# VectorE's order within a step of the dense layers, and PSUM banks of their own for the first step's last products

## The chip, the cores and the metric

The kernel runs on one core of a Trainium2 chip. The metric is the time of one execution on the device in microseconds (us); several executions are timed, and their median counts. TensorE is called PE below (its weight loads PEld), VectorE DVE, ScalarE ACT, GpSimd POOL, SyncE SP.

## The reference

Three stages, one after the other: a block attention over 2 x 768 tokens, a mixture of 8 experts (512 to 1024 to 512), and two dense layers with a piecewise quadratic gate between them. The change lies in the third stage alone:

```python
def _moe2_ref(x, w_in, w_out):            # x 1536 x 512, w_in 512 x 2048, w_out 2048 x 512
    h = x @ w_in
    neg = h <= -1.0
    pos = h >= 1.0
    g = np.where(pos, h, np.where(neg, 0.0, (h + 1.0) ** 2 / 4.0))
    return g @ w_out
```

## The kernel before

The dense layers begin 333.5 us into the span, when the experts' last matmul has been issued, and run to its end. They go through 16 steps (the loop over `s` in `run`): steps 0 to 7 take eight pairs of 128 hidden features for the first 768 tokens, steps 8 to 15 the same pairs for the other 768.

**Products.** A step computes 256 features of h for 768 tokens as a 2 x 2 by 2 x 2 block product with seven products in place of eight (the Strassen-Winograd scheme). Each is six matmuls (L1010) of 128 x 384, since every operand is split into a high part (`ah`, `yh`) and a remainder (`al`, `yl`). Product j of a step goes into a PSUM tile `ph`, of which there are two. Products 0, 1, 4 and 6 begin a tile; 2 adds onto 0's, 3 onto 1's, 5 onto 4's. So between them stand readers:

- `x1` (ACT, L1130) copies product 0; product 2 may write onto it only then.
- `u2` (DVE, L1132) is product 1 plus x1; product 3 may write only then.
- `u3` (DVE, L1132) is products 1 and 3 plus x1. Product 4 takes the tile that u3 has read.
- c22 (DVE, L1139) is product 4 plus u3; product 5 may write only then. c12 is product 5's tile plus u2, c21 is product 6 plus u3. c11 is product 0's tile after product 2, with no add.

**Gates.** Each of c11, c22, c12, c21 then passes through `gate`, a generator in three parts: relu and square on ACT (L1018, L1019); a clamp on DVE (L1021) and the high part `gh` on ACT (L1023); the remainder `gl` on DVE (L1026). `advance()` runs the next part of every open gate. It is called once for each product, so a gate's parts are issued one product apart or more.

**Outer products.** After each product, five (after the last six) matmuls of 128 x 512 (L1043) of the step before are issued: `gh` and `gl` times the split rows of w_out (`wh`, `wl`), added up over eight steps in six PSUM tiles `po0` to `po5`. These and the two `ph` fill PSUM. The four blocks of a step are used up in the order c11 (`po0` to `po2`), c12 (`po3` to `po5`), c21, c22.

**The other work in a step.** DVE makes four sums of w_in's blocks for the next step (`sums`, L977: S0 to S3 below, 128 x 256 each); ACT and POOL split the seven left operands of the next step (`side`, `ah` L987, `al` L988), where sides 1, 3, 4 and 5 read S1, S2, S0 and S3; `split` makes `wh` on ACT and `wl` on DVE (steps 0 to 5) or POOL (from step 6 on; L1001). In steps 1 to 6 `fill` converts the weights that are still missing from 64-bit to 32-bit floats, three DVE operations (L931, L933, L935) for each half tile, seven operations in a step; the third one issues the next load on SP. Step 6 also makes four combinations of the second half's tokens on DVE (`second`, L1075 to L1081), and step 7 splits them (`renew`, ACT L1088 and DVE L1090; the last one in step 8). In step 8 the first half's results are stored.

Nothing is scheduled by a planner: each engine executes its instructions in the order in which this Python code issues them. For steps 1 to 15 that order on DVE is, by product (work that a step doesn't have falls out):

| product | DVE, in order |
|---|---|
| 0 | gl(c12), clamp(c21) of the step before; S0, S1, S2, S3; one fill |
| 1 | u2; gl(c21); one fill |
| 2 | one fill |
| 3 | u3; clamp(c11); one fill |
| 4 | c22; gl(c11); wl of the first half; one fill |
| 5 | c12; clamp(c22); one fill |
| 6 | c21; gl(c22), clamp(c12); wl of the second half; one fill |

Of the kernel before, what the change touches and what calls it, by code (L numbers as in the profile page):

```python
# [8 lines left out]
F32 = mybir.dt.float32  # L9
# [4 lines left out]
OP = mybir.AluOpType  # L14
# [4 lines left out]
B, H, S, D = 2, 8, 768, 64  # L19
# [24 lines left out]
HALF = 384  # L44
# [759 lines left out]
def run_experts(router, ex, ff, plan=PLAN):  # L804
# [67 lines left out]
    for n, _ in enumerate(run):  # L872
        if n % TAIL == 0:
            next(conversions, None)
# [3 lines left out]
class FeedForward:  # L878
# [89 lines left out]
        sub(self.L[:, 3:7, :, v], R[:, :, :, at + 96:at + 192], self.H[:, 3:7, :, v].bitcast(F32))  # L968
        return todo

    def sums(self, p):

        nc, S, a = self.nc, self.S, self.pair(p)
        a11, a12, a21, a22 = (a[:, i, 256 * c:256 * c + 256] for i in range(2) for c in range(2))
        for j, (x, y, op) in enumerate(((a21, a22, OP.add), (S[:, 0], a11, OP.subtract), (a11, a21, OP.subtract),
                                        (a12, S[:, 1], OP.subtract))):
            nc.vector.tensor_tensor(S[:, j], x, y, op=op)  # L977

    def side(self, s, j):

# [10 lines left out]
    def split(self, s, i):  # L991

        nc = self.nc
        x = self.pair(s % self.PAIRS)[:, i, 512:]
        h = self.ww.tile([128, 512], F32R, name="wh")
        l = self.ww.tile([128, 512], F32R, name="wl")
        self.W[s, i] = h, l
        nc.scalar.activation(h, x, AF.Copy)
        if s < 6:
            yield  # L1000
        (nc.vector if s < 6 else nc.gpsimd).tensor_tensor(l, x, h.bitcast(F32), op=OP.subtract)  # L1001

    def product(self, s, j, p, first):

# [87 lines left out]
    def run(self, ctx):  # L1092
        nc, tc = self.nc, self.tc
# [10 lines left out]
        x1, u2, u3 = (self.st.tile([128, HALF], F32, name=n) for n in ("x1", "u2", "u3"))  # L1104
        P = self.PAIRS
        lower, upper = range(3), range(3, 6)
        order = ((0, 0, lower), (0, 1, upper), (1, 0, lower), (1, 1, upper))
        gates, renewed, rest = [], iter(()), iter(())

        def advance():  # L1110
            for g in list(gates):
                if next(g, 0) == 0:
                    gates.remove(g)

        for s in range(2 * P):
            outer = self.outer(s - 1, order) if s else iter(())
            for j, (_, kind) in enumerate(self.STEPS):
                if j in (0, 1, 4, 6):
                    p = self.pp.tile([128, HALF], F32, name="ph")
                    first = True  # L1120
                    if j == 0:
                        px = p
                    elif j == 1:
                        py = p
                else:
                    p = {2: px, 3: py, 5: p}[j]
                    first = False
                self.product(s, j, p, first)
                if j == 0:
                    nc.scalar.activation(x1, p, AF.Copy)  # L1130
                elif kind in ("u2", "u3"):
                    nc.vector.tensor_tensor(u2 if kind == "u2" else u3, p, x1, op=OP.add)  # L1132
                elif kind == "c11":
                    advance()
                    gates.append(self.gate((s, 0, 0), p))
                    next(gates[-1])
                else:
                    c = self.wk.tile([128, HALF], F32, name="c")
                    nc.vector.tensor_tensor(c, p, u2 if kind == "c12" else u3, op=OP.add)  # L1139
                    advance()  # L1140
                    gates.append(self.gate((s, int(kind[1]) - 1, int(kind[2]) - 1), c))
                    next(gates[-1])
                if j in (0, 1, 3):
                    advance()
                next(rest, None)
                for _ in range((12 if j == 6 else 4) if s == 2 * P - 1 else (6 if j == 6 else 5)):
                    next(outer, None)
                if s + 1 < 2 * P:
                    if j == 0:
                        while self.done < min(4 * (s + 1) + 2, len(self.halves)) and s + 1 < P:  # L1150
                            next(self.fill)
                        self.sums((s + 1) % P)
                    self.side(s + 1, j)
                if j in (3, 5):
                    while self.done < 4 * s + 4 and s < P:
                        next(self.fill)
                    rest = self.split(s, j // 5)
                    next(rest, None)
                if s:
                    next(self.fill, None)  # L1160
                if s == P - 2 and j in (1, 3, 5, 6):
                    self.second((1, 3, 5, 6).index(j))
                next(renewed, None)
                if s == P - 1:
                    renewed = self.renew(j)
                    next(renewed)
        for _ in range(2):
            advance()
        for t in (3, 4, 5, 0, 1, 2):
            h = t // 3  # L1170
# [59 lines left out]
```

## Time and profile before

| | us |
|---|---|
| median of 3 runs | 607.24 (605.71 to 609.76) |
| the profiled execution: its time | 608.52 |
| the profiled execution: its span, first to last instruction | 606.7 |
| of it before the dense layers' first matmul | 333.5 |

All times of rows below are from the start of the span of this one execution. A stall of an engine is the idle time ahead of an instruction; the profile names what ended it. A matmul row's length is longer than its pitch, since matmuls overlap: 128 x 384 matmuls start 0.17 to 0.18 us apart when nothing holds them. A row marked `[0.65 <-DVE u L1132]` had 0.65 us of idle time before it, which ended with that DVE operation.

### The profile page before, as it was taken

Reading aid. Unit: us, or ns where it says so; the run is one execution under the profiler, and the core shown is the slowest. Engines: PE = TensorE matmul, PEld = TensorE weight load, DVE = VectorE, ACT = ScalarE, POOL = GpSimd, SP = SyncE. Lnnn points to the kernel's source line nnn. Section 1 sums busy time; section 2 is a strip of 40 time slices with the busy share of each in tenths; the row PEclk is TensorE's granted clock in tenths of the full one; section 3 lists DMA queues with packets and bytes.
Section 4 is the critical chain, followed back from the end, with each engine's and each line's share of the span. In section 5 each row is a group of like instructions: output and inputs, shape, how many; then the busy total and the mean of one; then the engine's idle time right before and its main releaser. Section 6 shows DMA issues by size and latency. Waiting matters only on the chain.

```text
span 606.7 us, 11467 instructions
## 1 busy us (share of the span) xinstructions
PE 578.9 (95%) x4316; PEld 486.5 (80%) x4316; DVE 422.7 (70%) x1094; ACT 277.4 (46%) x645; POOL 176.6 (29%) x273
## 2 busy tenths in 40 slices
PE   6799998999999999999999889999999999999996
PEld 4568683478888888899999778888787889888884
DVE  6887865753664656620888799999999677777761
ACT  5666660021222222222321765556578566666653
POOL 5412100110101101110400333343365575555534
PEclk9999998999999999999999999999999899999999
DMA  9999023497837539498567222221000110000002
GB/s 214 185 202 205 26 89 123 62 314 231 273 92 244 197 108 284 167 184 228 189 222 245 54 70 70 70 79 61 1 0 1 68 38 2 0 1 0 2 1 104
DMA packets 84073, 71.42 MB, mean 118 GB/s; under 512 B 42546, under 2 KB 71218, under 8 KB 84018
## 3 DMA queue, kind: packets, MB, share of 16 engines
q1 hardware_dynamic: 81506, 64.38, 39.2%
q0 software_dynamic: 1984, 6.29, 3.7%
q8 instruction: 34, 0.56, 0.4%
q14 instruction: 21, 0.17, 0.1%
q10 hardware_dynamic: 528, 0.02, 0.0%
HBM read 64.38 MB, written 6.30 MB: 116 GB/s over the span
## 4 chain that ended last, share of the span: by engine, by line
PE 73%; DVE 18%; ACT 3%; issue 3%; POOL 1%; DMA 0%; POOLq 0%; DVEq 0%
PE acc L783 15%; PE acc L792 15%; PE ph L1010 14%; PE po L1043 11%; DVE sums L977 2%; PE rt L566 2%; DVE u L1021 2%; PE px L716 2%; PE po L313 2%; DVE gl L1026 2%; PE pt L299 2%; PE ps L275 2%; DVE u L1132 1%; DVE slot L933 1%; PE ptr L168 1%
## 5 line engine op out<-in xcount | busy, mean ns | idle before, releaser
L783 PE MATMUL acc<-xt,slot 128*128 128x192 f32 x512 | 95.5, 334 | 0.6 <-ACT xt L765 0.6
L792 PE MATMUL acc<-ht,slot 128*128 128x192 f32 x512 | 94.7, 333 | 0.0
L1010 PE MATMUL ph<-yh,ah 128*128 128x384 f32 x224 | 78.8, 352 | 9.4 <-DVE u L1132 7.7
L783 PEld LDWEIGHTS acc<-xt,slot 128*128 128x128 f32 x512 | 82.1, 190 | 1.7 <-ACT xt L765 0.8
L792 PEld LDWEIGHTS acc<-ht,slot 128*128 128x128 f32 x512 | 82.3, 190 | 0.8
L988 POOL TENSOR_TENSOR al<-sums,ah 128x256 fp32r<-128x256 f32 x64 | 53.4, 835 | 80.8 <-ACT ah L987 64.8
L1010 PE MATMUL ph<-yh,al 128*128 128x384 f32 x224 | 75.8, 338 | 0.0
L1043 PE MATMUL po<-wh,gh 128*128 128x512 f32 x192 | 75.8, 395 | 0.0
L1043 PE MATMUL po<-wl,gh 128*128 128x512 f32 x192 | 75.8, 395 | 0.0
L1043 PE MATMUL po<-wh,gl 128*128 128x512 f32 x192 | 75.5, 393 | 0.0
L1010 PE MATMUL ph<-yl,ah 128*128 128x384 f32 x224 | 75.5, 337 | 0.0
L988 POOL TENSOR_TENSOR al<-slot,ah 128x256 fp32r<-128x256 f32 x48 | 43.2, 900 | 100.3 <-ACT ah L987 92.7
L724 POOL DMA_INDIRECT xg<-xdram,idx x16 | 15.0, 936 | 184.1 <-ACT idx L695 94.3
L1023 ACT ACTIVATE gh<-u 128x384 fp32r<-128x384 f32 x64 | 33.6, 525 | 73.1 <-DVE u L1021 72.6
L1010 PEld LDWEIGHTS ph<-yh,ah 128*128 128x128 f32 x224 | 42.2, 188 | 22.3 <-DVE u L1132 16.3
L1026 DVE TENSOR_TENSOR gl<-u,gh 128x384 fp32r<-128x384 f32 x64 | 50.6, 791 | 4.7 <-ACT gh L1023 4.7
L787 ACT ACTIVATE ht<-acc 128x192 f32<-128x192 f32 x64 | 21.1, 330 | 66.6 <-PE acc L783 66.6
L1010 PEld LDWEIGHTS ph<-yl,ah 128*128 128x128 f32 x224 | 42.3, 189 | 3.2
L1139 DVE TENSOR_TENSOR c<-ph,u 128x384 f32<-128x384 f32 x48 | 26.7, 556 | 26.0 <-PE ph L1010 25.3
L1010 PEld LDWEIGHTS ph<-yh,al 128*128 128x128 f32 x224 | 42.2, 189 | 0.0
L1043 PEld LDWEIGHTS po<-wh,gl 128*128 128x128 f32 x192 | 36.2, 189 | 6.1 <-DVE gl L1026 0.4
L1043 PEld LDWEIGHTS po<-wh,gh 128*128 128x128 f32 x192 | 36.4, 189 | 5.1
(228 smaller groups left out, 998.6 us busy)
## 6 DMA issues: line engine op xcount, KB each, us to landing
slot<-in_moe_w_dram SPq DMA_DIRECT2D x31, 1024.0 KB, 8.8
raw<-in_moe_w_in_dram SPq DMA_DIRECT2D x16, 512.0 KB, 4.1
raw<-in_moe_w_out_dram SPq DMA_DIRECT2D x16, 512.0 KB, 3.4
vw<-in_v_dram SPq DMA_DIRECT2D x20, 192.0 KB, 5.2
nat<-in_k_dram SPq DMA_DIRECT2D x12, 256.0 KB, 4.7
nat<-in_q_dram SPq DMA_DIRECT2D x12, 256.0 KB, 5.4
xdram<-xs SPq DMA_DIRECT2D x12, 256.0 KB, 3.1
slot<-in_moe_w_dram SPq DMA_DIRECT2D x2, 512.0 KB, 3.5
```

Of the source, the lines that this page charges most:

```text
L275: nc.tensor.matmul(s[a][64 * w:64 * w + 64, c], QT[b * G + i // 2][r, c, n:n + 64], KW[b][r, i // 2, c, n // 64], start=False, stop=True, ...
L299: nc.tensor.transpose(pt[:, c], pr[:, c], ident)
L724: nc.gpsimd.indirect_dma_start(out=self.XG[k][:, h], out_offset=None, in_=self.x, in_offset=bass.IndirectOffsetOnAxis(ap=idx[:, h:h + 1], ...
L783: nc.tensor.matmul(p, w[:, c, f % 4 * 128:f % 4 * 128 + 128], xt[:, c], start=(c == 0), stop=(c == 3))
L787: nc.scalar.activation(ht[:, f], p, AF.Relu)
L792: nc.tensor.matmul(p, w[:, f, c % 2 * 128:c % 2 * 128 + 128], ht[:, f], start=(f == 0), stop=(f == 7))
L988: nc.gpsimd.tensor_tensor(l, x, h.bitcast(F32), op=OP.subtract)
L1010: nc.tensor.matmul(p, w[:, 128 * c:128 * c + 128], y[:, b, c], start=first and n == 0, stop=n == 5, skip_group_check=True)
L1023: nc.scalar.activation(gh, u, AF.Copy)
L1026: nc.vector.tensor_tensor(gl, u, gh.bitcast(F32), op=OP.subtract)
L1043: nc.tensor.matmul(self.po[t], x[:, c], w, start=(self.left[t] == 6 * self.PAIRS - 1), stop=(self.left[t] == 0))
L1139: nc.vector.tensor_tensor(c, p, u2 if kind == "c12" else u3, op=OP.add)
```

## The change

`sums` can issue some of its four operations. In `run`:

- S0, S1, S2, S3 are issued at products 0, 1, 3 and 5, no longer all at product 0; a side waits in the loop until its sum has been issued.
- `advance()` comes behind u2 and u3 as before, but ahead of the c22, c12 and c21 adds, no longer behind them.
- c21's gate is only put on the list at product 6; its relu and square are issued by the next step's first `advance()`, its clamp at product 1, its gl at product 2. After the loop there are three rounds of `advance()` in place of two.
- The seven fills of a step are issued 1, 0, 3, 1, 1, 1, 0 by product in place of one each.
- Step 0 takes its products in the order 0, 1, 4, 2, 3, 5, 6; products 4, 5 and 6 go into `po3`, `po4` and `po5`, with no adding of 5 onto 4. c12 is then made by two adds (product 4 plus u2 ahead of time, later product 5). Both `wl` of step 0 are made on POOL, and `split` comes at the third and the fifth product.
- Step 1 uses up step 0's blocks in the order c11, c22, c12, c21, so that `po3` to `po5` are first needed for c22.

On DVE, steps 1 to 15 then have this order:

| product | DVE, in order |
|---|---|
| 0 | gl(c12) of the step before; S0; one fill |
| 1 | u2; clamp(c21); S1 |
| 2 | gl(c21); three fills |
| 3 | u3; clamp(c11); S2; one fill |
| 4 | gl(c11); c22; wl of the first half; one fill |
| 5 | clamp(c22); c12; S3; one fill |
| 6 | gl(c22), clamp(c12); c21; wl of the second half |

```diff
--- before.py
+++ after.py
@@ -968,13 +968,14 @@
         sub(self.L[:, 3:7, :, v], R[:, :, :, at + 96:at + 192], self.H[:, 3:7, :, v].bitcast(F32))
         return todo
 
-    def sums(self, p):
-
-        nc, S, a = self.nc, self.S, self.pair(p)
+    def sums(self, p, which=range(4)):
+
+        S, a = self.S, self.pair(p)
         a11, a12, a21, a22 = (a[:, i, 256 * c:256 * c + 256] for i in range(2) for c in range(2))
-        for j, (x, y, op) in enumerate(((a21, a22, OP.add), (S[:, 0], a11, OP.subtract), (a11, a21, OP.subtract),
-                                        (a12, S[:, 1], OP.subtract))):
-            nc.vector.tensor_tensor(S[:, j], x, y, op=op)
+        todo = ((a21, a22, OP.add), (S[:, 0], a11, OP.subtract), (a11, a21, OP.subtract), (a12, S[:, 1], OP.subtract))
+        for j in which:
+            x, y, op = todo[j]
+            self.nc.vector.tensor_tensor(S[:, j], x, y, op=op)
 
     def side(self, s, j):
 
@@ -996,9 +997,9 @@
         l = self.ww.tile([128, 512], F32R, name="wl")
         self.W[s, i] = h, l
         nc.scalar.activation(h, x, AF.Copy)
-        if s < 6:
+        if 0 < s < 6:
             yield
-        (nc.vector if s < 6 else nc.gpsimd).tensor_tensor(l, x, h.bitcast(F32), op=OP.subtract)
+        (nc.vector if 0 < s < 6 else nc.gpsimd).tensor_tensor(l, x, h.bitcast(F32), op=OP.subtract)
 
     def product(self, s, j, p, first):
 
@@ -1105,6 +1106,7 @@
         P = self.PAIRS
         lower, upper = range(3), range(3, 6)
         order = ((0, 0, lower), (0, 1, upper), (1, 0, lower), (1, 1, upper))
+        first = ((0, 0, lower), (1, 1, upper), (0, 1, upper), (1, 0, lower))
         gates, renewed, rest = [], iter(()), iter(())
 
         def advance():
@@ -1112,59 +1114,76 @@
                 if next(g, 0) == 0:
                     gates.remove(g)
 
+        def block(s, key, p, other):
+
+            c = self.wk.tile([128, HALF], F32, name="c")
+            nc.vector.tensor_tensor(c, p, other, op=OP.add)
+            if key is None:
+                return c
+            gates.append(self.gate((s,) + key, c))
+            if key != (1, 0):
+                next(gates[-1])
+
         for s in range(2 * P):
-            outer = self.outer(s - 1, order) if s else iter(())
-            for j, (_, kind) in enumerate(self.STEPS):
-                if j in (0, 1, 4, 6):
-                    p = self.pp.tile([128, HALF], F32, name="ph")
-                    first = True
-                    if j == 0:
-                        px = p
-                    elif j == 1:
-                        py = p
+            outer = self.outer(s - 1, first if s == 1 else order) if s else iter(())
+            ph, sided, summed = {}, 0, 0
+            for n, j in enumerate((0, 1, 4, 2, 3, 5, 6) if s == 0 else range(7)):
+                if s == 0 and j > 3:
+                    ph[j] = self.op.tile([128, 512], F32, name=f"po{j - 1}")[:, :HALF]
+                elif j in (0, 1, 4, 6):
+                    ph[j] = self.pp.tile([128, HALF], F32, name="ph")
                 else:
-                    p = {2: px, 3: py, 5: p}[j]
-                    first = False
-                self.product(s, j, p, first)
+                    ph[j] = ph[{2: 0, 3: 1, 5: 4}[j]]
+                p = ph[j]
+                self.product(s, j, p, j in (0, 1, 4, 6) or s == 0 and j == 5)
                 if j == 0:
                     nc.scalar.activation(x1, p, AF.Copy)
-                elif kind in ("u2", "u3"):
-                    nc.vector.tensor_tensor(u2 if kind == "u2" else u3, p, x1, op=OP.add)
-                elif kind == "c11":
-                    advance()
+                elif j in (1, 3):
+                    nc.vector.tensor_tensor(u2 if j == 1 else u3, p, x1, op=OP.add)
+                advance()
+                if j == 2:
                     gates.append(self.gate((s, 0, 0), p))
                     next(gates[-1])
-                else:
-                    c = self.wk.tile([128, HALF], F32, name="c")
-                    nc.vector.tensor_tensor(c, p, u2 if kind == "c12" else u3, op=OP.add)
-                    advance()
-                    gates.append(self.gate((s, int(kind[1]) - 1, int(kind[2]) - 1), c))
-                    next(gates[-1])
-                if j in (0, 1, 3):
-                    advance()
+                elif s:
+                    if j > 3:
+                        block(s, {4: (1, 1), 5: (0, 1), 6: (1, 0)}[j], p, u2 if j == 5 else u3)
+                elif j == 4:
+                    part = block(s, None, p, u2)
+                elif j == 5:
+                    block(s, (0, 1), p, part)
+                elif j == 3:
+                    block(s, (1, 1), ph[4], u3)
+                elif j == 6:
+                    block(s, (1, 0), p, u3)
                 next(rest, None)
-                for _ in range((12 if j == 6 else 4) if s == 2 * P - 1 else (6 if j == 6 else 5)):
+                for _ in range((12 if n == 6 else 4) if s == 2 * P - 1 else (6 if n == 6 else 5)):
                     next(outer, None)
                 if s + 1 < 2 * P:
-                    if j == 0:
+                    if n == 0:
                         while self.done < min(4 * (s + 1) + 2, len(self.halves)) and s + 1 < P:
                             next(self.fill)
-                        self.sums((s + 1) % P)
-                    self.side(s + 1, j)
-                if j in (3, 5):
+                    more = (1, 2, 2, 3, 3, 4, 4)[n]
+                    self.sums((s + 1) % P, range(summed, more))
+                    summed = more
+                    while sided < 7 and (sided == 0 or (s, sided - 1) not in self.A) and (
+                            s == 0 or sided <= n) and (0, 2, 0, 3, 1, 4, 0)[sided] <= summed:
+                        self.side(s + 1, sided)
+                        sided += 1
+                if n in ((3, 5) if s else (2, 4)):
                     while self.done < 4 * s + 4 and s < P:
                         next(self.fill)
-                    rest = self.split(s, j // 5)
+                    rest = self.split(s, n // (5 if s else 4))
                     next(rest, None)
                 if s:
-                    next(self.fill, None)
-                if s == P - 2 and j in (1, 3, 5, 6):
-                    self.second((1, 3, 5, 6).index(j))
+                    for _ in range((1, 0, 3, 1, 1, 1, 0)[n]):
+                        next(self.fill, None)
+                if s == P - 2 and n in (1, 3, 5, 6):
+                    self.second((1, 3, 5, 6).index(n))
                 next(renewed, None)
                 if s == P - 1:
                     renewed = self.renew(j)
                     next(renewed)
-        for _ in range(2):
+        for _ in range(3):
             advance()
         for t in (3, 4, 5, 0, 1, 2):
             h = t // 3
```

## Rows read from the trace of the kernel before

**Rows 1.** First part of the page: busy time, share of the span, instructions.

```profile
PE 578.9 (95%) x4316; PEld 486.5 (80%) x4316; DVE 422.7 (70%) x1094; ACT 277.4 (46%) x645; POOL 176.6 (29%) x273
```

**Rows 2.** PE's waits in the dense layers: us in total, times, longest.

```profile
PE ph L1010 <- DVE u L1132: 7.7, 12, 1.8
PE ph L1010 <- ACT x L1130: 0.7, 1, 0.7
PE ph L1010 <- DVE c L1139: 0.7, 1, 0.7
```

**Rows 3.** Windows, steps 0, 1, 2-5, 6-7, 8, 9, 10, 11-14: length, busy, PEclk, DMA.

```profile
333.54:342.88 9.34, 8.04 (x44) 7.39 (x43) 6.70 (x15) 5.54 (x13) 3.48 (x5) 1.00 0.38 94
342.88:361.32 18.44, 16.18 (x80) 13.98 (x79) 16.07 (x29) 12.01 (x27) 6.39 (x9) 1.00 0.18 58
361.32:427.86 66.54, 64.60 (x314) 55.90 (x312) 62.35 (x105) 40.34 (x89) 24.61 (x29) 1.00 0.20 64
427.86:461.98 34.12, 32.37 (x158) 27.96 (x156) 32.64 (x48) 22.75 (x48) 17.62 (x17) 1.00 0.00 1
461.98:481.60 19.62, 17.72 (x79) 15.29 (x78) 14.05 (x22) 12.71 (x29) 10.85 (x14) 0.91 0.05 18
481.60:497.75 16.15, 15.90 (x79) 14.05 (x78) 12.89 (x20) 10.81 (x25) 12.67 (x19) 1.00 0.21 78
497.75:513.38 15.63, 15.63 (x80) 14.13 (x78) 11.49 (x18) 10.17 (x23) 8.45 (x10) 1.00 0.01 2
513.38:576.85 63.47, 63.47 (x313) 56.17 (x312) 47.70 (x69) 40.14 (x89) 33.90 (x37) 1.00 0.00 1
```

**Rows 4.** PE's timeline in step 0, product 3 to 4: start, length.

```profile
337.71 0.34 PE L1010 MATMUL ph<-yh,al 128*128 128x384 f32 x1
338.69 0.44 PE L1010 MATMUL ph<-yh,ah 128*128 128x384 f32 x1 [0.65 <-DVE u L1132]
```

**Rows 5.** Timeline of step 3: u2, product 3, u3, product 4.

```profile
384.49 0.54 DVE L1132 TENSOR_TENSOR u<-ph,x 128x384 f32<-128x384 f32 x1
385.08 0.44 PE L1010 MATMUL ph<-yh,ah 128*128 128x384 f32 x1 [0.31 <-DVE u L1132]
...
387.29 0.55 DVE L1132 TENSOR_TENSOR u<-ph,x 128x384 f32<-128x384 f32 x1
...
387.89 0.44 PE L1010 MATMUL ph<-yh,ah 128*128 128x384 f32 x1 [0.34 <-DVE u L1132]
```

**Rows 6.** DVE's waits in steps 2 to 4 (361.32 to 411.14), all of them.

```profile
DVE c L1139 <- PE ph L1010: 2.9, 6, 0.7
```

**Rows 7.** Forms of four lines: ns min/median/max, first and last start, shapes.

```profile
L977 DVE TENSOR_TENSOR sums<-slot x32: 410/420/970, 293.3 to 565.4; 128x256 f32<-128x256 f32 x32
...
L935 DVE SCALAR_TENSOR_TENSOR slot<-raw,slot x32: 677/691/1225, 290.8 to 437.2; 128x512 int32<-128x512 int32 x32
...
L1026 DVE TENSOR_TENSOR gl<-u,gh x64: 541/550/1880, 340.5 to 594.2; 128x384 fp32r<-128x384 f32 x64
...
L1001 POOL TENSOR_TENSOR wl<-slot,wh x20: 1285/1309/2015, 440.4 to 591.2; 128x512 fp32r<-128x512 f32 x20
```

**Rows 8.** Timeline of step 11 around product 4: PE, ACT, POOL, DVE.

```profile
522.42 0.34 PE L1010 MATMUL ph<-yh,ah 128*128 128x384 f32 x1
522.53 0.53 ACT L1023 ACTIVATE gh<-u 128x384 fp32r<-128x384 f32 x1 [2.05 <-DVE u L1021]
...
523.44 0.74 POOL L988 TENSOR_TENSOR al<-sums,ah 128x256 fp32r<-128x256 f32 x1 [2.15 <-ACT ah L987]
...
523.67 0.56 DVE L1139 TENSOR_TENSOR c<-ph,u 128x384 f32<-128x384 f32 x1 [1.18 <-PE ph L1010]
...
524.15 1.71 DVE L1026 TENSOR_TENSOR gl<-u,gh 128x384 fp32r<-128x384 f32 x1
```

**Rows 9.** Timeline of step 6, DVE behind u3 and clamp(c11).

```profile
438.71 0.94 DVE L1077 TENSOR_TENSOR yr<-yr 128x768 f32<-128x768 f32 x1
```

**Rows 10.** PE's timeline in step 8, first matmul of product 3.

```profile
470.90 0.44 PE L1010 MATMUL ph<-yh,ah 128*128 128x384 f32 x1 [1.78 <-DVE u L1132]
```

## Prediction

> **What bounds the kernel now.** The first part of the page comes first: PE is busy 579 of 607 us, DVE 423 [rows 1]. So the matmuls set the time, and a change on DVE can only win back what PE waits. The change lies in the dense layers, so the next view is PE's waits there: nearly all end with one line, L1132, that is u2 or u3 [rows 2]. The windows by step tell where [rows 3]. Step 10 is 15.63 us long and PE is busy in all of it; I take that as a step without a stall. What the others have above it: step 1 2.81, steps 2 to 5 66.54 - 4 x 15.63 = 4.02, steps 6 and 7 2.86, step 8 3.99, step 9 0.52, steps 11 to 14 63.47 - 62.52 = 0.95. Step 0 has no outer products: in it the last matmul of product 3 starts at 337.71, the next at 338.69 [rows 4], 0.98 in place of 0.17 to 0.18, so 0.8 lost, and 0.1 by a slower restart. The second stall of that step, before L1139, is as long (0.7 idle against 0.65) [rows 2, 4]: 1.8 together. In all 17 us, 2.8% of the time: no reordering can give more.
>
> Why u2 is late is seen in step 3: PE goes on 0.05 us after the end of u2, and 0.05 after the end of u3 [rows 5]. The engine is not idle ahead of them: in steps 2 to 4 DVE waits 2.9 us in all, each time ahead of a c add [rows 6], never ahead of u2 or u3. The queue ahead of them is simply too long: before u2 stand gl, a clamp, four sums and a fill, 0.42 to 0.69 each [rows 7], while the c adds come when their product does.
>
> **The change part by part.** A product with its outer matmuls takes 15.63/7 = 2.2 us. A reader can start 1.25 after its product's first matmul (522.42 to 523.67 [rows 8]). So from a step's start u2 can start at 3.45 and is needed by 6.0; u3 at 7.85, needed by 8.2; c22 at 10.05, needed by 10.4. u2 has 2.5 us of room, the two others 0.35.
>
> *Step 0.* Products 4 to 6 write banks that nothing in the step reads first; 2 comes two products after x1's source, 3 three products after u2's. Both stalls go: **-1.8**. If the banks, last used by the experts, or a late u3 cost one of them, -0.9. DVE loses two wl and gains one add. The two wl take 2 x 1.3 on POOL [rows 7], which is busy 3.48 of 9.34 there [rows 3]; the first is needed only after 8 us, so nothing is charged; without that cover it would be 1.3.
>
> *Step 1.* Before step 1's x1 ACT now has a chain: c22's clamp stands ahead of the c12 add, c12's clamp ahead of the c21 add, and gh(c12) ahead of x1. From u3 (6.1 after step 0's start) that is five DVE operations of 0.55 and, on ACT, two gates' relu, square and gh, a wh and three ah, at about 0.5 each; with waits x1 ends near 12.5, where PE wants it at 7.4 + 2 x 2.2 = 11.8. So x1's wait (0.7 now [rows 2]) stays. u2 is then in time, but three fills follow, and u3 may be a us late. I take **-0.2** of the 2.81, between +1.0 and -1.5.
>
> *Steps 2 to 5.* Ahead of u2 disappear the clamp (0.55), three sums (1.3) and a fill (0.4 to 0.7): 2.3 to 2.6 us, more than the stall; u2 is in time. What moves goes into the room behind it: between u2 and u3 now clamp(c21) 0.55, S1 0.42, gl(c21) 0.55, three fills 1.8, together 3.3 against 7.85 - 4.0 = 3.85. Each operation on two SBUF tensors can be held by POOL (a sum 0.97 in place of 0.42, gl up to 1.88 [rows 7]); two such holds make u3 about 0.3 late. Ahead of c22 come S2 and gl(c11), 0.9 us more: clamp(c11) ends 1.0 after u3's start, S2 and a fill take 1.0, gl 0.5, so c22 starts at 10.35 of 10.4. DVE's load sets a bound too: steps 2 to 4 last 49.82 us, less 2.9 idle [rows 6], 15.6 per step, as much as PE's 15.63. A step can lose the waits, but any new wait on DVE shows. I leave 0.45 of the mean 1.0: **-2.2**, between -0.5 and -3.6.
>
> *Steps 6 and 7.* u2's and u3's waits shrink as above (-2.3). But `second` and `renew` put an operation of 0.94 [rows 9] between clamp(c11) and gl(c11), so gl is 0.9 later, when POOL's al and wl hold it, and c22 now stands behind gl: 0.7 to 2.1 in each (a hold by both, 1.71 instead of 0.55 [rows 8], plus the operation). I take 1.0 each: **-0.3**, between +2.0 and -2.0.
>
> *Step 8.* The longest wait, 1.78, was u2's [rows 10]; three sums and a clamp leave its queue, 1.8 to 2.9 us, and x1 comes ahead of c21's relu and square. The granted clock of this step is 0.91 [rows 3], so 0.09 x 19.62 = 1.8 of its 3.99 is PE at the lower of its two levels (1.2 of 2.4 GHz). The waits, 2.2, go. The drop began at that wait, but step 1, with 2.8 us of stalls, ran at clock 1.00 [rows 3], so it needn't go with the wait; I count it as gone: **-3.7**, -2.0 if it stays.
>
> The Trainium skill ("TensorE: Matmul & The Clock Gate", Part 1) says that the array's clock is throttled by default and activity releases it. By that rule this drop follows the wait and goes with it, as I counted; by the row of step 1 alone it might have come anyway, and the sum would be 1.8 less.
>
> *Steps 9, 11 to 14.* All waits there are u2's, without fills: -0.4 and **-0.9**. *The loads and the outer products.* The third operation of a fill issues a load on SP; with three fills in a row it goes out a product earlier or later, but the loaded tile is needed nine fills, over a step of 15.6 us, later. Nothing else stands on SP there. c21's gate ends one product later, at product 2; its first outer matmul is the fourth after product 3, 2 us behind. In step 1 c22 is wanted second, by the last outer matmul after product 1, at 7.4 + 2.2 + 2.1 = 11.7 from step 0's start; its gh is due near 9.7, by the chain above. All three at nothing; without the cover DVE would stop at the head of a fill with u3 behind it, or PE in an outer product, about 1 us each.
>
> *Step 15* has four outer matmuls per product, so c22 behind gl is 0.1 late: **+0.1**. The end (36 outer matmuls, the last store) keeps its length: PE has no gap there, and c21's later gate is needed last of all.
>
> The sum: -1.8 - 0.2 - 2.2 - 0.3 - 3.7 - 0.4 - 0.9 + 0.1 = **-9.4**, against the profiled execution's own 608.52 (span 606.7 and 1.8 around it): 599.1. That execution lies 1.3 above the median of 607.24; if the drop of the clock is what sets it apart, 1.8 of the gain isn't to be had there: 607.24 - 7.6 = 599.6. I take 599.3.
>
> **The rivals.** *All waits go.* If POOL's holds fall where DVE has room, steps 0 to 14 lose nearly all 17 us: 608.5 - 13.9 (the sum of the better ends) = 594.6. For it: 2.9 us of idle DVE before c adds is filled. Against: DVE's 15.6 us in a step.
>
> *Given back in the same step.* The three fills ahead of u3 and gl ahead of c22 cost what u2 gains, so steps 1 to 7 keep their length. What is left: -1.8 - 2.0 (or 3.7) - 0.4 - 0.9 = -5.1 to -6.8, so 602 to 603.5; with 0.3 more lost in each of them 604 to 605.5. For it: both have 0.35 us of room.
>
> *c22 behind a held gl: slower.* In steps 6 to 14 POOL's al and then wl start right after gh(c11) [rows 8]. Now gl(c11) can start at 523.12 (gh ends 523.06), al at 523.44: gl is first by 0.3. If POOL is first, gl ends when wl has ended, as it did at 525.86, and c22 starts then, not at 523.67: 1.8 us past the 0.35 of room that it has. Nine steps of it are 16, and in steps 1 to 5, where al alone holds, 0.6 each: 19 in all, of which 2 are in the sum: 608.5 - 9.4 + 17 = 616. It decides at gl(c11) becoming ready 0.3 us later than here, or ah 0.3 earlier. Against it: ACT makes ah after gh, so the order is fixed where DVE is free.
>
> The Trainium skill ("GPSIMD Engine Reference", Key points) says that POOL shares its SBUF interfaces with DVE and contends with instructions that have two SBUF inputs, with no exception for the one that came first. By that rule gl would be slowed at each meeting, in 15 steps, which goes toward this rival; the rows show reads of PSUM at 0.54 to 0.56 throughout [rows 5, 8], and gl at 0.55 in the median [rows 7], so mostly it isn't met.
>
> *It doesn't do what it says.* Step 0's new banks or POOL's wl come late and step 1 grows by what step 0 won: 601.
>
> **How the numbers follow.** Forecast (597 to 602) 0.52; all waits go 0.20; given back 0.19; doesn't do what it says 0.03; held gl 0.06. About 1% (6 us, 601.2 to 613.3) is what a measurement of this kernel tells from no change. Faster: 0.43 of the forecast, 0.20 and 0.01; within: 0.09, 0.19 and 0.02; slower: 0.06. The range that leaves out the two worst tenths runs from the first rival's 594.6, taken down to 594, to the second's 604.5.
>
> **What the profile would show.** Step 0: 42 product matmuls without a gap, step 1 starting 7.4 us after it. L1001 on POOL 22 times, on DVE 10. L1132's row among PE's waits falls from 7.7 to under 3, and what is left ends with u3 (product 4), not u2. DVE's idle time moves from the c adds to u2 and u3. The forecast is wrong if L1139 (c22) appears among PE's waits at product 5 with over 0.3 us per step, if u3 is late by more than u2 gained, or if the clock drops again elsewhere in the dense layers.

## The result and the profile after

The changed kernel takes 600.81 us in the median of four runs (598.72 to 602.05), the kernel before 607.12 in four runs (605.71 to 609.76): a ratio of 0.9888 with an interval of 0.9844 to 0.9931, 1.1% faster. The forecast was 599.3 in a range of 594.0 to 604.5. The profiled execution after took 602.05 with a span of 600.2. In the changed kernel line numbers are shifted: the product matmuls are L1011, u2 and u3 L1142, x1 L1140, the c adds L1120, the clamp L1022, gl L1027, the sums L978, wl L1002.

First part of the page of the kernel after, to be laid beside [rows 1]: PE is busy 1.9 us less, DVE 17 us less, though DVE's work is the same up to two `wl` that went to POOL and one add more in step 0.

```profile
PE 577.0 (96%) x4311; PEld 487.8 (81%) x4316; DVE 405.8 (68%) x1093; ACT 278.0 (46%) x645; POOL 176.7 (29%) x275
```

Windows of the kernel after, by the steps of [rows 3]: step 0, 1, 2 to 5, 6 and 7, 8, 9, 10, 11 to 14.

```profile
335.25:342.76 7.51, 7.51 (x45) 7.51 (x43) 4.99 (x12) 4.53 (x11) 4.25 (x5) 1.00 0.60 149
342.76:363.66 20.90, 17.77 (x79) 15.35 (x79) 18.85 (x33) 14.26 (x32) 9.18 (x11) 0.92 0.14 51
363.66:427.60 63.94, 63.86 (x313) 56.06 (x312) 57.65 (x105) 40.31 (x88) 22.98 (x28) 1.00 0.21 67
427.60:460.86 33.26, 32.06 (x158) 28.01 (x157) 30.44 (x47) 23.30 (x49) 16.80 (x17) 1.00 0.00 1
460.86:476.48 15.62, 15.62 (x79) 14.12 (x78) 13.82 (x21) 12.14 (x26) 10.24 (x13) 1.00 0.06 23
476.48:492.33 15.85, 15.85 (x80) 14.05 (x78) 12.14 (x18) 9.61 (x22) 13.03 (x18) 1.00 0.21 79
492.33:507.96 15.63, 15.63 (x80) 14.13 (x79) 11.10 (x20) 11.49 (x27) 9.55 (x11) 1.00 0.00 1
507.96:570.46 62.50, 62.50 (x313) 56.50 (x312) 39.16 (x69) 40.15 (x89) 32.92 (x37) 1.00 0.00 1
```

With the lengths of [rows 3] subtracted, step by step: step 0 -1.83, **step 1 +2.46**, steps 2 to 5 -2.60, steps 6 and 7 -0.86, step 8 -4.00, step 9 -0.30, steps 11 to 14 -0.97; what follows step 14 0.1 to 0.2 less. That is -8.2 from the dense layers' first matmul to the end of the span (273.2 to 265.0), while the two profiled executions differ by 6.5. The other 1.7 lie before the dense layers, which begin at 335.25 in place of 333.54 though the change touches nothing there. A stretch of the experts, after:

```profile
96.00:112.00 16.00, 14.55 (x100) 5.34 (x101) 9.64 (x57) 0.38 (x1) 0.00 (x0) 0.68 0.07 29
```

and the same stretch of the kernel before:

```profile
96.00:112.00 16.00, 14.27 (x119) 5.96 (x119) 10.90 (x62) 0.65 (x3) 0.00 (x0) 0.89 0.17 62
```

The clock stands at 0.68 there against 0.89, and fewer matmuls get done. Over the four runs of the kernel after the time goes with the granted clock: 598.72 at 0.995, 602.05 at 0.986. So steps are compared below, which begin and end inside the dense layers.

PE's waits in the dense layers after, beside [rows 2]: u's row went from 7.7 us in 12 waits to one wait of 2.3, and the c adds now wait twice.

```profile
PE ph L1011 <- DVE u L1142: 2.3, 1, 2.3
PE ph L1011 <- DVE c L1120: 1.1, 2, 0.7
PE ph L1011 <- ACT x L1140: 0.9, 1, 0.9
```

Step 3 after, beside [rows 5]: DVE around u2 (383.10) and u3 (387.96), and the weight load and the matmul that begin product 4.

```profile
383.10 0.56 DVE L1142 TENSOR_TENSOR u<-ph,x 128x384 f32<-128x384 f32 x1 [1.36 <-PE ph L1011]
...
385.20 1.23 DVE L933 SCALAR_TENSOR_TENSOR slot<-raw,slot 128x512 int32<-128x512 int32 x1
386.46 0.69 DVE L935 SCALAR_TENSOR_TENSOR slot<-raw,slot 128x512 int32<-128x512 int32 x1
387.07 0.97 DVE L931 TENSOR_SCALAR slot<-raw 128x512 int32<-128x512 int32 x1
387.96 0.55 DVE L1142 TENSOR_TENSOR u<-ph,x 128x384 f32<-128x384 f32 x1
...
388.56 0.19 PEld L1011 LDWEIGHTS ph<-yh,ah 128*128 128x128 f32 x1 [0.44 <-DVE u L1142]
...
388.56 0.44 PE L1011 MATMUL ph<-yh,ah 128*128 128x384 f32 x1
```

u2 is no longer late: DVE itself stood idle for 1.36 us until product 1 was done. u3 comes right behind three fills, and PE goes on just after it. This small stall isn't in the list of PE's waits at all; it is the **weight load** that is charged with it. In steps 2 to 5 the list of the weight loads' waits reads:

```profile
PEld ph L1011 <- DVE u L1142: 1.8, 4, 0.4
PEld ph L1011 <- DVE c L1120: 0.6, 2, 0.3
```

Step 1 after: u2 (349.77), product 3's first matmul (350.53), the three fills, u3 (354.56) and product 4, which waited 2.25.

```profile
349.77 0.54 DVE L1142 TENSOR_TENSOR u<-ph,x 128x384 f32<-128x384 f32 x1
...
350.53 0.34 PE L1011 MATMUL ph<-yh,ah 128*128 128x384 f32 x1
...
351.93 1.24 DVE L935 SCALAR_TENSOR_TENSOR slot<-raw,slot 128x512 int32<-128x512 int32 x1
...
353.09 0.41 DVE L931 TENSOR_SCALAR slot<-raw 128x512 int32<-128x512 int32 x1
...
353.54 1.09 DVE L933 SCALAR_TENSOR_TENSOR slot<-raw,slot 128x512 int32<-128x512 int32 x1
354.56 0.54 DVE L1142 TENSOR_TENSOR u<-ph,x 128x384 f32<-128x384 f32 x1
...
355.15 0.64 PE L1011 MATMUL ph<-yh,ah 128*128 128x384 f32 x1 [2.25 <-DVE u L1142]
```

From u2 to u3 DVE takes as long as in step 3 (4.79 and 4.86 us). What differs is where u2 stands: 0.76 ahead of product 3 in step 1, 3.08 ahead in step 3 (product 3 starts at 386.18 there). Without that lead three fills push u3 past PE by over 2 us. And behind the wait the clock fell; a stretch of 2.3 us that begins 1 us later:

```profile
356.20:358.50 2.30, 2.30 (x8) 2.01 (x8) 1.83 (x4) 1.22 (x3) 1.06 (x1) 0.50 0.36 132
```

0.50 is the lower of the two levels; over the step the clock is 0.92, so it cost 0.08 x 20.9 = 1.7 us more.

Step 6 after, around product 5:

```profile
437.30 0.95 DVE L1078 TENSOR_TENSOR yr<-yr 128x768 f32<-128x768 f32 x1
...
437.99 0.86 POOL L989 TENSOR_TENSOR al<-sums,ah 128x256 fp32r<-128x256 f32 x1 [2.42 <-ACT ah L988]
438.17 1.09 DVE L1027 TENSOR_TENSOR gl<-u,gh 128x384 fp32r<-128x384 f32 x1
...
439.19 0.55 DVE L1120 TENSOR_TENSOR c<-ph,u 128x384 f32<-128x384 f32 x1
...
439.79 0.44 PE L1011 MATMUL ph<-yh,ah 128*128 128x384 f32 x1 [0.68 <-DVE c L1120]
```

L1078 delays gl(c11), gl runs beside POOL's al and takes 1.09 in place of 0.55, and c22 stands behind it: the chain of the forecast, with 1.1 us of PE's waits in steps 6 and 7.

### The profile page after: what moved, and what is told of

It is laid out like the page before. It is cut to its first block, busy times and chain, and to the rows that moved or that the text cites. A ratio compares the mean times of both kernels' runs of the same rounds, so it can differ in the third digit from the quotient of the medians.

```text
span 600.2 us, 11447 instructions
## 1 busy us (share of the span) xinstructions
PE 577.0 (96%) x4311; PEld 487.8 (81%) x4316; DVE 405.8 (68%) x1093; ACT 278.0 (46%) x645; POOL 176.7 (29%) x275
## 4 chain that ended last, share of the span: by engine, by line
PE 85%; DVE 7%; issue 2%; ACT 2%; POOL 1%; DMA 0%; POOLq 0%; DVEq 0%
PE po L1044 18%; PE ph L1011 18%; PE acc L783 15%; PE acc L792 15%; PE px L716 3%; PE rt L566 2%; PE po L313 2%; PE pt L299 2%; PE ps L275 2%; PE ptr L168 1%; PE ptr L207 1%; PE rt L687 1%; PE ptr L341 1%; PE px L764 1%; POOL out_dram L1062 1%
## 5 line engine op out<-in xcount | busy, mean ns | idle before, releaser
L1011 PE MATMUL ph<-yh,ah 128*128 128x384 f32 x218 | 75.8, 348 | 4.4 <-DVE u L1142 2.3
L1011 PE MATMUL ph<-yh,al 128*128 128x384 f32 x218 | 73.9, 339 | 0.0
L1011 PE MATMUL ph<-yl,ah 128*128 128x384 f32 x218 | 73.6, 338 | 0.0
L989 POOL TENSOR_TENSOR al<-slot,ah 128x256 fp32r<-128x256 f32 x48 | 41.5, 867 | 90.3 <-ACT ah L988 57.0
L1027 DVE TENSOR_TENSOR gl<-u,gh 128x384 fp32r<-128x384 f32 x64 | 50.1, 782 | 7.9 <-ACT gh L1024 7.4
L1011 PEld LDWEIGHTS ph<-yh,ah 128*128 128x128 f32 x218 | 41.1, 189 | 13.2 <-DVE u L1142 5.1
L1011 PEld LDWEIGHTS ph<-yl,ah 128*128 128x128 f32 x218 | 41.2, 189 | 3.5
L1011 PEld LDWEIGHTS ph<-yh,al 128*128 128x128 f32 x218 | 41.2, 189 | 0.0
L1044 PEld LDWEIGHTS po<-wl,gh 128*128 128x128 f32 x192 | 36.2, 189 | 5.0
```

What stands on the lines that cost most here:

```text
L989: nc.gpsimd.tensor_tensor(l, x, h.bitcast(F32), op=OP.subtract)
L1011: nc.tensor.matmul(p, w[:, 128 * c:128 * c + 128], y[:, b, c], start=first and n == 0, stop=n == 5, skip_group_check=True)
L1027: nc.vector.tensor_tensor(gl, u, gh.bitcast(F32), op=OP.subtract)
L1044: nc.tensor.matmul(self.po[t], x[:, c], w, start=(self.left[t] == 6 * self.PAIRS - 1), stop=(self.left[t] == 0))
```

## The experiments

All kernels but the sixth are the changed kernel with an edit; the sixth is the kernel before with one. Medians in us, ratios to the kernel before, run beside each (its interval in brackets), and the length of the steps in the profile (the eighth, with added work, is told below). In rows of kernels 1, 2, 5, 6, 8 and 9 u2 and u3 are L1144; x1 is L1142 in these but for the eighth, where it is L1140.

| kernel | median | ratio | step 0 | 1 | 2-5 | 6-7 | 8 | 9 | 11-14 |
|---|---|---|---|---|---|---|---|---|---|
| before | 607.12 | | 9.34 | 18.44 | 66.54 | 34.12 | 19.62 | 16.15 | 63.47 |
| after | 600.81 | 0.9888 [0.9844, 0.9931] | 7.51 | 20.90 | 63.94 | 33.26 | 15.62 | 15.85 | 62.50 |
| 1 step 0 only | 606.25 | 0.9979 [0.9958, 1.0001] | 7.52 | 19.20 | 66.52 | 34.10 | 18.07 | 16.14 | 63.48 |
| 2 later steps only | 597.75 | 0.9861 [0.9822, 0.9901] | 9.34 | 17.59 | 63.94 | 33.26 | 15.62 | 15.82 | 62.51 |
| 3 fills even | 595.17 | 0.9816 [0.9779, 0.9852] | 7.52 | 17.98 | 62.52 | 33.25 | 15.63 | 15.81 | 62.50 |
| 4 step 1's fills | 597.59 | 0.9856 [0.9818, 0.9894] | 7.53 | 17.70 | 65.69 | 33.25 | 15.63 | 15.83 | 62.51 |
| 5 adds first | 594.35 | 0.979 [0.9766, 0.9813] | 7.53 | 17.84 | 62.50 | 32.70 | 15.76 | 15.77 | 62.50 |
| 6 sums alone | 596.71 | 0.982 [0.9795, 0.9844] | 9.37 | 16.92 | 62.50 | 32.29 | 16.33 | 16.06 | 62.51 |
| 7 sums at once | 598.5 | 0.9852 [0.9829, 0.9875] | 7.50 | 19.22 | 62.50 | 32.49 | 17.09 | 17.47 | 62.51 |
| 9 combined | 594.93 | 0.9809 [0.978, 0.9837] | 7.52 | 17.26 | 63.36 | 33.04 | 15.63 | 15.63 | 62.51 |

**1 and 2: the change in two halves.** In the first kernel step 0 is new and steps 1 to 15 keep the old order; in the second it is the other way round. The core of the first:

```diff
+            if s:
+                advance()
             if key is None:
                 return c
...
-            if key != (1, 0):
+            if s or key != (1, 0):
...
-                advance()
+                if not (s and j > 3):
+                    advance()
...
-                    more = (1, 2, 2, 3, 3, 4, 4)[n]
+                    more = 4 if s else (1, 2, 2, 3, 3, 4, 4)[n]
...
-                    for _ in range((1, 0, 3, 1, 1, 1, 0)[n]):
+                    for _ in range(1):
```

> Step 0 as in the change, steps 1 to 15 in the old order. Theory (step 0 wins its two waits; step 1 lost 2.5 us because three fills stand ahead of u3, and the clock fell behind that wait): step 0 7.5 us; with the old order there are only two fills between u2 and u3, so step 1 is 18.4 to 19.5 us long, at clock 1.00; steps 2 to 14 as before; 605 to 606.5 us. Rival (step 1 is long because step 0 is shorter and ACT's chain runs into it, whatever the fills do): step 1 20.5 us or more, nothing left of step 0's gain, 607 or more.

> Step 0 as before, steps 1 to 15 in the new order. Theory: step 0 9.3 us; in step 1 the three fills still stand ahead of u3, so step 1 stays near 18.5 us (product 4 waits over 1 us for u3); steps 2 to 15 as in the changed kernel, 8.6 us less than before; 598.5 to 600 us. Rival (step 0's shortening is what made step 1 long): step 1 is 16.5 to 17 us long without a wait for u3 over 0.5, 597 us.

Step 0's new banks win their 1.82 with the old order behind them too, but step 1 then takes 0.76 more than before. That fits longer queues left to it by a shorter step 0, which is argued here and not tested. In the second half alone step 1 takes 17.59 with the three fills in it, between the theory and its rival; its product 4 waits 0.62, not 2.25:

```profile
352.28 0.44 PE L1011 MATMUL ph<-yh,ah 128*128 128x384 f32 x1 [0.62 <-DVE u L1144]
```

So step 1's loss of 2.46 needs both halves, and the second half alone isn't slower than the whole change.

Step 8 of the first kernel, with its u2's wait, and the whole step's window:

```profile
468.15 0.44 PE L1011 MATMUL ph<-yh,ah 128*128 128x384 f32 x1 [1.77 <-DVE u L1144]
```

```profile
459.21:477.28 18.07, 16.16 (x79) 13.98 (x78) 13.96 (x22) 12.74 (x29) 11.28 (x14) 1.00 0.05 19
```

This is the wait of [rows 10] in the old order, 1.77 beside 1.78, but with the clock at 1.00. So the drop doesn't have to follow it. It also splits step 8's 3.99: 18.07 - 15.63 = 2.44 are waits, 19.62 - 18.07 = 1.55 the clock.

**3 and 4: the fills.** The third kernel issues one fill per product, as before; the fourth only in step 1 moves the three fills behind u3.

```diff
-                    for _ in range((1, 0, 3, 1, 1, 1, 0)[n]):
+                    for _ in range(1):
```

```diff
-                    for _ in range((1, 0, 3, 1, 1, 1, 0)[n]):
+                    for _ in range(((1, 0, 0, 1, 2, 2, 1) if s == 1 else (1, 0, 3, 1, 1, 1, 0))[n]):
```

> The changed kernel with one fill after each product. Theory (sums, clamp and adds in their new order free u2, the fills' places matter little from step 2 on): steps 2 to 5 within 0.3 us per step of the changed kernel's 16.0; in step 1 two fills stand ahead of u3 in place of three, so its wait falls from 2.3 to about 1; 599 to 600.5 us. Rival (the fills' move made the gain of steps 2 to 7): steps 2 to 5 go back to 16.6 us each, 602 to 603.5 us.

> The changed kernel with step 1's seven fills issued 1, 0, 0, 1, 2, 2, 1 by product, so that none stands between u2 and u3. Theory: product 4 of step 1 waits under 0.3 us in place of 2.3, the clock stays at 1.00 in steps 0 to 15, step 1 is 16.8 to 17.3 us long in place of 20.9; 596.5 to 598 us. Rival 1 (step 0's shortening): step 1 over 19.5 us. Rival 2 (the drop of the clock comes of itself): step 1 or another of the dense layers' steps shows a granted clock under 0.95 without a wait over 1.5 us; 598.5 us or more.

Windows of the third kernel, step 1 and steps 2 to 5:

```profile
339.54:357.52 17.98, 16.31 (x80) 13.86 (x79) 17.46 (x32) 13.97 (x32) 9.15 (x11) 1.00 0.16 59
357.52:420.04 62.52, 62.52 (x314) 56.50 (x312) 55.47 (x105) 40.53 (x89) 23.39 (x28) 1.00 0.21 68
```

It is faster than either theory had it: step 1 loses 2.9 us against the changed kernel, and steps 2 to 5 lose 1.4 more and have no stall at all. So with the rest of the change in place, the fills' move was a loss in steps 1 to 5.

The fourth kernel came out at the time expected, but not by the steps expected. u3 is in time in step 1, yet product 5 waits 0.66 there for c22, so the step takes 17.70 and not 17.3 or less; and step 1 handed u3's wait on. Step 2's window and its product 4:

```profile
357.41:375.09 17.68, 15.91 (x79) 14.04 (x78) 17.36 (x31) 11.01 (x25) 6.88 (x8) 1.00 0.32 102
```

```profile
368.14 0.44 PE L1011 MATMUL ph<-yh,ah 128*128 128x384 f32 x1 [1.77 <-DVE u L1142]
```

Step 2's own three fills stand ahead of its u3, now behind DVE's work that step 1 put off: DVE is busy 17.36 of the 17.68. In steps 1 and 2 together the kernel wins 36.82 - 35.38 = 1.4 over the changed one, no more than the drop of the clock.

**5: the c adds first again.** Even fills, and from step 1 on the c adds ahead of the gates' parts, as before the change.

```diff
             nc.vector.tensor_tensor(c, p, other, op=OP.add)
+            if s:
+                advance()
...
-                advance()
+                if not (s and j > 3):
+                    advance()
```

> The changed kernel with even fills, and in steps 1 to 15 the c22, c12 and c21 adds ahead of the older gates' parts again. Theory (in steps 6 and 7 c22 is late because it stands behind gl(c11), which POOL holds): product 5's waits of 0.95 in step 6 and 0.61 in step 7 go, the last step loses its 0.1, nothing else moves by more than 0.2; steps 6 and 7 together 31.6 to 32 us in place of 33.25; 593 to 594 us. Rival (the adds' place behind the gates' parts is what empties the queue ahead of u2): waits at product 3 come back in steps 2 to 9, 0.2 to 0.5 each; 596 us or more.

PE's waits in its dense layers:

```profile
PE ph L1011 <- DVE u L1144: 1.7, 3, 0.8
PE ph L1011 <- ACT x L1142: 0.9, 1, 0.9
```

The waits for a c add are gone, so gl ahead of c22 was their cause, but in their place PE waits 0.33 and 0.56 for u3 in steps 6 and 7. Of the 2.0 us that the two steps had above 2 x 15.63, 0.55 are won. No wait at product 3 came back, so the rival fell; its 594.35 us lie just above the range expected. This is the lowest median of all the kernels, 2.1% below the one before, though not clear of the third and the ninth.

**6 and 7: the reliefs apart.** The sixth is the kernel before with the sums spread and nothing else; the core of its edit, set against the kernel before, comes first. The seventh has even fills and all four sums at product 0 again, which leaves c21's later gate and the order of adds as reliefs; these two were not run apart with the sums in their old place.

```diff
-                        self.sums((s + 1) % P)
-                    self.side(s + 1, j)
+                    more = (1, 2, 2, 3, 3, 4, 4)[n]
+                    self.sums((s + 1) % P, range(summed, more))
+                    summed = more
+                    while sided < 7 and (sided == 0 or (s, sided - 1) not in self.A) and (
+                            sided <= n) and (0, 2, 0, 3, 1, 4, 0)[sided] <= summed:
+                        self.side(s + 1, sided)
+                        sided += 1
```

```diff
-                    more = (1, 2, 2, 3, 3, 4, 4)[n]
+                    more = 4 if s else (1, 2, 2, 3, 3, 4, 4)[n]
```

> The kernel before with the four sums spread over products 0, 1, 3 and 5 and nothing else. Theory (u2 is late because the queue ahead of it is too long, so taking three sums out is most of the cure): product 3's waits go in steps 2 to 9 and 11 to 14, product 4's waits stay under 0.3; steps 2 to 5 62.5 to 64 us in place of 66.5, steps 11 to 14 62.5; step 0 stays 9.3; 598 to 600 us. Rival (c21's later gate does it): product 3's waits shrink by less than half; 603 us or more.

> The changed kernel with even fills, but with all four sums at product 0 in steps 1 to 15. What is left of the change there is c21's later gate and the adds behind the gates' parts. Theory: the queue ahead of u2 is shorter by one clamp only (0.55 to 1.1); about half of product 3's waits of before come back, 0.2 to 0.4 in steps 2 to 5 and 1.0 to 1.5 in step 8; 598.5 to 600.5 us. Rival (c21's later gate does it): waits at product 3 stay under 0.1 everywhere; 595 to 596 us.

Steps 2 to 5 of the sixth kernel:

```profile
360.64:423.14 62.50, 62.50 (x313) 56.49 (x312) 56.39 (x105) 40.04 (x90) 23.12 (x29) 1.00 0.21 68
```

The seventh has no stall in these steps either (62.50), where its theory had half of the waits back. So the sums' move and the rest of the order each clear steps 2 to 5, and neither is "the" cause there: u2's queue was too long by less than each of them takes out of it. Elsewhere they differ, and the rival of the seventh fails: product 3 waits 1.41 in step 1 and 1.02 in step 8; with the sums at once step 1 is as long as in the first kernel (19.22 and 19.20; 17.98 with the sums spread), and steps 8 and 9 lose 1.5 and 1.8, most of it in waits for u2 and u3; in the sixth it is 0.7 and 0.4. The sums alone beat the whole change, against the expectation, since they bring neither the three fills nor a shorter step 0 ahead of an unready step 1.

**8: does a long wait bring the clock down?** Even fills, and copies of product 1 ahead of u2 as extra DVE work in three steps that have no stall otherwise: 8, 10 and 13 of them in steps 10, 12 and 14.

```diff
+                    for _ in range({10: 8, 12: 10, 14: 13}.get(s, 0) if j == 1 else 0):
+                        nc.vector.tensor_copy(u2, p)
                     nc.vector.tensor_tensor(u2 if j == 1 else u3, p, x1, op=OP.add)
```

> The changed kernel with even fills, and in steps 10, 12 and 14 eight, ten and thirteen copies of product 1 ahead of u2 on DVE (0.5 us each, overwritten by u2), so that PE waits at product 3 about 1.3, 2.3 and 3.7 us. If the granted clock falls behind such a wait of PE, all three or the longer ones show 0.5 for some us after the wait, costing 1.5 to 2 each above the wait; if the drop comes of itself, the clock stays at 1.00 in steps 9 to 15 or falls elsewhere.

One execution was taken, of 611.65 us. The waits came out longer than meant. They and the three steps' windows:

```profile
496.07 0.45 PE L1011 MATMUL ph<-yh,ah 128*128 128x384 f32 x1 [2.40 <-DVE u L1144]
531.19 0.44 PE L1011 MATMUL ph<-yh,ah 128*128 128x384 f32 x1 [3.29 <-DVE u L1144]
569.35 0.61 PE L1011 MATMUL ph<-yh,ah 128*128 128x384 f32 x1 [5.06 <-DVE u L1144]
```

```profile
486.91:505.51 18.60, 16.17 (x79) 13.98 (x78) 15.76 (x27) 11.00 (x26) 9.20 (x10) 1.00 0.00 0
521.14:541.89 20.75, 17.46 (x79) 15.34 (x78) 15.84 (x28) 10.03 (x23) 8.15 (x10) 0.92 0.00 1
557.52:580.03 22.51, 17.45 (x79) 15.44 (x78) 17.12 (x31) 9.98 (x23) 8.15 (x10) 0.92 0.00 1
```

The two longer waits are followed by a step at 0.92, the one of 2.40 by a step at 1.00. In this one execution, then, PE's own stall did bring the clock down, and it cost as much after 3.29 as after 5.06: 20.75 - 15.63 - 3.29 is 1.8, 22.51 - 15.63 - 5.06 is 1.8, while 18.60 - 15.63 - 2.40 is 0.6 without a drop: 1.2 for the clock.

**9: the pieces together.** Adds first (by the fifth kernel's edit, not shown again), step 1's fills behind u3, the sums at once in step 7 alone, c21's gate of step 5 begun at once.

```diff
-                    more = (1, 2, 2, 3, 3, 4, 4)[n]
+                    more = 4 if s == 7 else (1, 2, 2, 3, 3, 4, 4)[n]
...
-            if key != (1, 0):
+            if key != (1, 0) or s == 5:
...
-                    for _ in range((1, 0, 3, 1, 1, 1, 0)[n]):
+                    for _ in range((1, 0, 0, 1, 1, 2, 2)[n] if s == 1 else 1):
```

> The changed kernel with the c adds ahead of the gates' parts (from step 1 on), one fill after each product (in step 1 1, 0, 0, 1, 1, 2, 2), all four sums of step 7 at its product 0, and c21's gate of step 5 begun at once. Theory (each of the waits that are left comes from what stands between u2 and u3 on DVE): step 1 about 17.0 us with x1's wait alone, steps 2 to 5 62.5, step 6 15.8, step 7 16.0; from the dense layers' first matmul to the last 252.3 us, 592.5 to 593 us. Rival (what leaves step 1 comes back in step 2, as it did with its fills put off): step 2 16.3 us or more, 594 us.

It took 594.93, no better than the fifth kernel, and the rival came true: step 1 is 0.58 shorter than there, but step 2 has a wait of 0.58 at product 4 instead (16.48 us in all), and step 7's product 4 waits 1.23.

## Why the prediction came out right, and which terms were off

**The main reason holds.** u2 was late since DVE's queue ahead of it was too long. With less ahead of it, of PE's twelve waits for u2 and u3 [rows 2] one is left, and DVE now idles ahead of u2; in steps 2 to 4 its waits read, beside [rows 6]:

```profile
DVE u L1142 <- PE ph L1011: 3.8, 3, 1.4
DVE gl L1027 <- ACT gh L1024: 0.8, 3, 0.3
```

That is the predicted move of DVE's idle time from the c adds to u2; none of it went to u3, which the forecast had named as well. **Step 0** (-1.8, measured -1.83), **step 9** (-0.4, -0.30) and **steps 11 to 14** (-0.9, -0.97) came as worked out.

**Step 8** (-3.7, measured -4.0): waits and the clock both went, and the run of the first half split them at 2.44 and 1.55. The forecast's own parts, 2.2 and 1.8, make 4.0 as well; no reason is given for the 3.7. Whether the drop "needn't go with the wait" was rightly left open: in all profiles of the study the clock is below 1.00 between the dense layers' first and last matmul only in a step with a PE stall of 1.78 or more, yet stalls of 1.77 (twice) and 2.40 left it at 1.00, and 1.78, 2.25, 3.29 and 5.06 didn't. The Trainium skill ("TensorE: Matmul & The Clock Gate", Part 1) has the clock throttled by default and released by activity; the runs agree as far as every drop in these layers lies behind a stall, but don't follow it for each stall.

The single executions on record say more. The kernel before was run 29 times beside the experiments; with the same code its granted clock over a whole execution goes from 1.000 (606.42 us) to 0.984 (609.66 us). Step 8's drop alone takes 0.09 x 19.62 of 606.7, that is 0.003, so in the execution at 1.000 it didn't come (its stalls aren't on record). It isn't the order of the work alone that brings the drop, and in an execution without it the 1.55 can't be won: the 599.6 that the forecast set beside its 599.1 allowed for that. Where the clock fell in an execution is known for the profiled ones alone.

**Step 1 is the step that failed:** "u2 is then in time, but three fills follow, and u3 may be a us late", -0.2 between +1.0 and -1.5. Measured: +2.46. u3's wait was 2.25, and the clock behind it cost 1.7, which the term didn't hold at all; without the drop it would have been +0.8. The mechanism was named, its size came from the wrong place: the three fills were priced at 1.8, by themselves, and took 2.6 to u3 (351.93 to 354.56), two of them held. And "u2 is in time" was true only just, with no lead that could pay for them. With the fills even step 1 is 17.98 (-0.46), inside the bounds. The charge of nothing for the two `wl` on POOL is in doubt too: S3 (344.72), on the way to step 1's x1, takes 1.57 us beside the second of them (344.70). But x1 is about as late with both `wl` on DVE (a wait of 0.85 in the sixth kernel, 0.88 here), so that isn't shown to cost anything.

**Steps 2 to 5** (-2.2, measured -2.60) are well forecast on an argument that is wrong in part. "DVE's load sets a bound": 15.6 us per step as if it were fixed. The same 105 operations take 62.35 us before, 57.65 after, 55.47 with the fills even. An operation's time depends on what POOL does meanwhile: in the dense layers of the kernel before no sum and no L931 that POOL leaves alone takes over 0.43 (26 of them), and beside a POOL operation they take up to 0.97. S3 took 0.96 in each of steps 2 to 5 before and takes 0.50 after (least, median and most of the four, in ns):

```profile
L977 DVE TENSOR_TENSOR sums<-slot,sums x4: 956/960/970, 365.9 to 415.7; 128x256 f32<-128x256 f32 x4
L978 DVE TENSOR_TENSOR sums<-slot,sums x4: 500/500/502, 376.9 to 424.9; 128x256 f32<-128x256 f32 x4
```

The Trainium skill ("GPSIMD Engine Reference", Key points) states that POOL contends with DVE instructions that have two SBUF inputs, as S3 has. The forecast counted such holds for single operations and not in the load. So *All waits go* was nearer than its chance of 0.20 said: its 594.6 is nearly reached by the changed kernel with even fills (595.17), and reached when the adds come first besides (594.35). What kept the change from it are the three fills, 2.9 us in step 1 and 1.4 in steps 2 to 5; for the latter "two such holds make u3 about 0.3 late" was right (0.35 per step).

**Steps 6 and 7** (-0.3, measured -0.86): the chain of L1078, gl and c22 is as described. It was priced at 1.0 for each step; PE's waits for c22 come to 1.1 in both together, so the term was 0.6 too bad. The rival that builds on it, a slower kernel, fell: outside these two steps gl(c11) isn't behind POOL where c22 needs it, and steps 8 to 14 have no such wait.

**The end** ("PE has no gap there") had one: a weight load waited 0.39 at 593.06 in the trace before for a gl, and doesn't after.

The sum was 1.2 too good for the dense layers (-9.4 and -8.2): step 1 was 2.7 worse than its term, the others 1.5 better. So the total came near in part by luck, since errors of opposite sign met. Of the signs listed ahead two came true against the forecast: c22 appeared at product 5 with over 0.3 (0.68 and 0.45, in steps 6 and 7 alone), and the clock dropped elsewhere. The third, u3 late by more than u2 gained, holds in step 1: 2.25 against the 1.60 that PE waited there for u2 in the kernel before.

Open: x1's wait in step 1, 0.7 to 0.9 in every kernel, has not been removed, and no placing of the fills was found that clears steps 1 and 2 together. What decides whether a stall of 1.8 to 2.4 us brings the clock down isn't settled. And how much of the seventh kernel's relief is c21's later gate, and how much the new place of the adds, was not measured.

## What to carry to other kernels

When an engine's order is changed in several ways at once, run its parts alone: here spreading the sums alone (596.7) beat the whole change (600.8), and one line of it, the three fills, cost 4.3 us in steps 1 to 5 of the profile, the drop of the clock included. Work that is moved out of one deadline's queue lands in the next one's, so look at the step where the lead is smallest, here the first one behind a shortened step, and not at the steady ones. A busy time that holds waiting for another engine is no load: look how the same operations vary before calling it a bound.

## What the hardware showed that was not expected

- DVE operations without a PSUM operand stretch while POOL works: in step 3 after, an L933 of 1.23 and an L931 of 0.97, which take 0.68 and 0.41 elsewhere; u2, u3 and the c adds, which read PSUM, stay at 0.54 to 0.56 in all rows here. Over four steps that makes 7 us of 62 in DVE's busy time.
- A stall of a few us in a PE that is busy otherwise can be followed by a stretch at 0.50, which costs some 1.2 to 1.7 us here whether the stall was 1.78 or 5.06 us; it came after 1.78 us once and not after 2.40, and not in every execution of the same kernel.
